# Two row tiles of a Fourier product taken by symmetry, through device memory, in batches 2 and 3

## The chip, the cores and the metric

The kernel runs on one core of one Trainium2 chip. The metric is the device time of one execution in microseconds (us), the median over runs. Before the change it is 284.78 us (three runs, 284.77 to 284.88). A difference of under 0.2% isn't told from no change.

The engines are named as in the profile: PE is TensorE (PEld its weight loads), DVE is VectorE, ACT is ScalarE, POOL is GpSimd, SP is the queue of SyncE, which here issues nearly all DMAs. Each engine runs its own instructions strictly in program order and waits at the first one whose inputs aren't ready.

## What is computed

Sparse causal attention over 4 batches of 8 heads (768 positions, head size 64), and then, for each batch, a Fourier mixing layer with an MLP:

```python
# x: (4, 768, 512), the attention's output with its heads side by side
X = np.fft.fft(x, axis=1)
X = np.fft.fft(X, axis=2)
mixed = np.real(X).astype(np.float32)
u = x + mixed
mu = np.mean(u, axis=-1, keepdims=True)
var = np.mean((u - mu) ** 2, axis=-1, keepdims=True)
un = (u - mu) / np.sqrt(var + 1e-06)
ch = np.maximum(un @ w_ch1, 0.0) @ w_ch2
return (u + ch).astype(np.float32)
```

Since `x` is real, the real part of its two-dimensional transform has a symmetry: `mixed[s, d]` equals `mixed[-s mod 768, -d mod 512]`. Row 768-s is row s with its columns 1 to 511 in reverse.

## The kernel before

The work is cut into small items, and a long string, `ORDER` (line 114), lists them one after another. The kernel walks through the list and issues the instructions of each item; so the list fixes, for each engine, the order of its own instructions. The table `WORK` (line 824) gives the function of each name. A second string, `PLACES` (line 185), says which of four PSUM buffers each new product takes, in the order in which the list makes them. An item that takes a buffer waits until the last reader of the product before it is done.

The 16 pairs of heads are numbered 0 to 15, four to a batch. A pair P goes through these items (the second number is a tile):

- `Lq`, `Lk`, `Lv`: loads on SP (line 284). `tq`, `tk` turn q and k, on PE for pairs 0 to 6 and on DVE from pair 7 on. `ks`, `kh` (block sums), `kc`, `qc`, `qs` (casts), `g` (gate scores on PE), `gt`, `gx`, `gl`, `gm` (the mask, on DVE), `K` (the mask put beside q, on POOL).
- `s:P,i`: a tile of scores on PE (line 483). `e:P,i`: its exp, on ACT (line 511). `d:P,i`: the causal diagonal, on POOL (line 519).
- `vc` (cast of v, POOL), `v:P` (attention times v, 42 matmuls, line 525), `x:P` (division into `x_b`, DVE).

A batch b is 768 rows, six row tiles of 128. After its four pairs it goes through these:

- `fs`, `fd`, `f`, `fc`: foldings of `x` on DVE and POOL. `y:b,h,gg`: the first Fourier product on PE (line 595). `ty:b,h`: its copy to SBUF, on ACT (line 614). `tr:b,h`: the same, turned, on DVE (line 622).
- `m:b,kp`: the second Fourier product, two row tiles (2 kp and 2 kp + 1) by eight matmuls of 256 columns (line 627). Row tiles 0 to 2 read `ty`, row tiles 3 to 5 read `tr`.
- `u:b,kt`: adds `x` to row tile kt of the product, into an fp32 tile in SBUF (DVE, line 640); it also sums the row. The three tiles of a batch, of two row tiles each, come from a ring of five buffers and later become the output.
- `nm:b,kt,n` (means of n row tiles, ACT), `xu:b,kt` (the centred row tile in fp16, ACT), `un:b,kt` (line 675: for batches 1 to 3 a transposing DMA on SP from `x_b` into `unT`), `bn`, `nv`, `nr` (the variance).
- `w:b,it`: a tile of the first MLP product on PE, over all 768 rows: for each of four slices of the inner dimension a matmul of 512 columns (row tiles 0 to 3) and one of 256 (row tiles 4 and 5) (line 709). `r:b,it`: its relu, on ACT or DVE (line 722). `c:b,st,h`: half of the second MLP product of row tile st, eight matmuls of 512 columns (line 731). `o` (DVE, line 753) adds it to `u`; `od` (SP, line 759) sends the row tile out.

While a batch is in its Fourier and MLP part, the pairs of the next batch fill the gaps. For batch 3 no pairs are left: between its Fourier product and its first `w` stand only the `c` items of batch 2.

Of the kernel before, what the change touches and what calls it, by code (L numbers as in the profile page):

```python
# [119 lines left out]
d:1,4 e:1,2 d:1,2 kc:4 kc:3 v:0 x:0 s:1,3 e:1,3 d:1,3 Lq:4 tq:4 qc:4 fs:0,1 s:2,2 g:3 s:1,5 e:2,2  # L120
gt:3 gx:3 gl:3,0 gl:3,1 s:2,1 e:1,5 Lv:1 vc:1 qs:4 s:2,5 e:2,1 d:1,5 d:1,1 d:2,2 e:2,5 d:1,0 d:2,5
g:4 gt:4 s:2,0 e:2,0 gx:4 gm:3 Lk:5 tk:5 s:2,3 ks:5 s:2,4 d:2,1 kh:5 d:2,0 e:2,3 d:2,3 Lq:5 tq:5
qc:5 qs:5 gl:4,0 fs:0,0 gl:4,1 Lv:2 e:2,4 d:2,4 vc:2 kc:5 v:1 x:1 s:3,2 e:3,2 Lv:3 vc:3 s:3,4 g:5
gt:5 gx:5 gm:4 fs:1,0 gl:5,0 e:3,4 d:3,4 s:3,3 s:3,0 e:3,0 s:3,5 e:3,5 d:3,5 d:3,2 d:3,0 e:3,3 d:3,3
v:2 gl:5,1 x:2 fs:2,0 fs:2,1 gm:5 fs:1,1 fd:2,1 fd:2,0 s:3,1 e:3,1 d:3,1 W:1 s:4,1 e:4,1 s:4,2 s:4,3
e:4,3 e:4,2 v:3 x:3 fs:3,1 fs:3,0 fd:3,1 fd:3,0 f:0,1 fc:0 f:0,0 s:4,5 s:5,2 e:5,2 e:4,5 d:4,5 s:4,0
e:4,0 d:4,0 s:5,0 e:5,0 LT:0 Lq:6 Lk:6 s:5,1 tk:6 ks:6 e:5,1 d:4,2 d:5,2 d:4,3 s:4,4 e:4,4 d:5,1
y:0,0,0 y:0,0,1 ty:0,0 kc:6 f:0,2 f:0,3 y:0,1,0 y:0,1,1 ty:0,1 tr:0,0 tr:0,1 s:5,3 e:5,3 s:5,4 e:5,4
LF:0 m:0,0 u:0,0 nm:0,0,1 xu:0,0 u:0,1 nm:0,1,1 m:0,2 s:5,5 e:5,5 u:0,4 nm:0,4,1 xu:0,1 u:0,5
nm:0,5,1 m:0,1 u:0,2 u:0,3 xt:0,0 tq:6 qc:6 xt:0,1 un:0,0 W:0 Lv:4 vc:4 d:4,1 kh:6 d:4,4 d:5,0 v:4  # L130
xu:0,4 xt:0,4 nm:0,2,1 xu:0,5 xt:0,5 un:0,2 g:6 gt:6 xu:0,2 nm:0,3,1 xu:0,3 xt:0,2 xt:0,3 w:0,6,2
# [745 lines left out]
```

## Time and profile before

| | before |
|---|---|
| median of the runs | 284.78 us |
| the profiled execution, its own time | 284.69 us |
| its span, from the first to the last instruction | 283.0 us |
| mean granted clock of TensorE | 0.999 |
| PE busy | 273.7 us, 2593 matmuls |
| DVE, ACT, POOL busy | 190.8, 166.3, 120.7 us |

How to read it: the profile's times count from the start of the span, so a term worked out from them is set against 283.0; the execution as a whole took 1.69 us more. The engines' busy times overlap. A line such as L636 is a line of the kernel; `out<-in` names what the instruction writes and reads, and x24 counts it. A group's line gives busy time, mean duration of one in ns, and behind the bar the idle time of the engine ahead of it with what ended it. A view by stretches gives the busy time of each engine between two moments. Matmuls are pipelined: one is shown for longer than it holds the engine, so the distance from a start to the next start is what it costs.

### The profile page before, as it was taken

The numbers are of one execution on the slowest core, as the hardware profiler recorded it, in microseconds if no ns is written. First come the engines' busy times: TensorE is split into PE (matmuls) and PEld (weight loads), VectorE is DVE, ScalarE is ACT, GpSimd is POOL, SyncE is SP. The second block draws the span as 40 slices with busy tenths as digits, with TensorE's granted clock in tenths as the row PEclk, the third lists the DMA queues.
The fourth block names the chain that finished last, engine by engine and source line by source line (L and its number), as shares of the span: only waits on it lengthen the run. The fifth ranks groups of instructions, "written<-read, shape, count | busy, mean of one in ns | idle before, by whom it ended". The sixth has DMA issues, their size and how long they took to land.

```text
span 283.0 us, 6718 instructions
## 1 busy us (share of the span) xinstructions
PE 273.7 (97%) x2593; PEld 170.0 (60%) x2593; DVE 190.8 (67%) x570; ACT 166.3 (59%) x222; POOL 120.7 (43%) x313
## 2 busy tenths in 40 slices
PE   7799998999999999999999999999999999999995
PEld 3567676876656646565665574566576555665453
DVE  2789998998899797998988669550376443380032
ACT  3599899668787269886497634669641261343100
POOL 2157839306895658747546538701522000002000
PEclk9999999999999999999999999999999999999999
DMA  7999999996999999459795152610000042000044
GB/s 179 231 218 212 222 189 154 182 189 115 156 136 203 150 131 211 63 107 193 153 205 108 28 161 74 120 71 0 0 3 2 30 110 46 2 37 0 2 166 169
DMA packets 119152, 33.45 MB, mean 118 GB/s; under 512 B 110736, under 2 KB 115920, under 8 KB 119120
## 3 DMA queue, kind: packets, MB, share of 16 engines
q1 hardware_dynamic: 113712, 28.43, 50.7%
q0 software_dynamic: 3664, 4.19, 9.6%
q10 hardware_dynamic: 1744, 0.40, 0.7%
q8 instruction: 20, 0.33, 0.5%
q14 instruction: 12, 0.10, 0.1%
HBM read 28.55 MB, written 6.29 MB: 123 GB/s over the span
## 4 chain that ended last, share of the span: by engine, by line
PE 81%; DVE 7%; DMA 3%; ACT 3%; POOL 3%; issue 2%; ACTq 0%; POOLq 0%; DVEq 0%
PE c L744 28%; PE h L719 28%; PE sc L499 7%; PE av L534 6%; PE yp L604 3%; ACT pt L516 2%; PE mx L636 2%; DMA nat<-in_k_dram 2%; PE mx L637 2%; DMA nat<-in_q_dram 1%; PE c L737 1%; DVE kr L362 1%; PE g L424 1%; PE sc L494 1%; POOL qk L246 1%
## 5 line engine op out<-in xcount | busy, mean ns | idle before, releaser
L516 ACT ACTIVATE pt<-sc 128x1024 f16<-128x1024 f32 (+1 forms) x96 | 82.8, 926 | 25.7 <-PE sc L499 17.5
L719 PE MATMUL h<-unT,w 128*128 128x256 f16 (+1 forms) x528 | 87.2, 321 | 0.0
L744 PE MATMUL c<-w_sb,hT 128*128 128x512 f16 x368 | 83.8, 379 | 0.0
L719 PEld LDWEIGHTS <-w 128*128 128x128 f16 x528 | 50.8, 98 | 31.0 <-issue 0.3
L744 PEld LDWEIGHTS <-hT 128*128 128x128 f16 x368 | 35.6, 98 | 40.2 <-issue 0.5
L729 ACT ACTIVATE hT<-h 128x768 f16<-128x768 f32 x48 | 37.8, 811 | 34.9 <-PE h L719 34.9
L522 POOL TENSOR_SCALAR_AFFINE_SELECT pt<-pt 128x256 f16<-128x256 f16 x96 | 38.0, 421 | 35.3 <-ACT pt L516 34.8
L756 DVE SCALAR_TENSOR_TENSOR u<-c,rs,u 128x512 f32<-128x512 f32 (+2 forms) x26 | 17.6, 702 | 36.4 <-PE c L744 33.3
L727 DVE TENSOR_SCALAR hT<-h 128x768 f16<-128x768 f32 x16 | 15.1, 951 | 22.0 <-PE h L719 21.9
L246 POOL TENSOR_SCALAR_AFFINE_SELECT qk<-mt 32x160 f16<-32x160 f16 x72 | 23.6, 348 | 14.1 <-DVE mt L471 12.6
L246 POOL TENSOR_SCALAR_AFFINE_SELECT qk<-q 64x768 f16<-64x768 f32 (+1 forms) x25 | 20.8, 832 | 18.8 <-DVE q L398 7.4
L499 PE MATMUL sc<-qk 96*128 96x512 f16 (+3 forms) x144 | 26.7, 306 | 0.0
L534 PEld LDWEIGHTS <-pt 128*128 128x128 f16 x672 | 22.2, 97 | 2.3 <-issue 0.7
L534 PE MATMUL av<-v,pt 128*128 128x65 f16 x672 | 23.0, 193 | 0.3 <-POOL v L246 0.3
L243 POOL TENSOR_TENSOR t<-vr,rs 128x6 f32<-128x6 f32 x12 | 2.7, 225 | 41.0 <-DVE rs L695 40.2
L499 PEld LDWEIGHTS <-qk 96*128 96x128 f16 x144 | 12.9, 98 | 9.2 <-issue 0.8
L246 POOL TENSOR_SCALAR_AFFINE_SELECT v<-nat 128x768 f16<-128x768 f32 x16 | 14.7, 922 | 5.2 <-DMA nat<-in_v_dram 5.1
L650 DVE SCALAR_TENSOR_TENSOR u<-mx,x 128x512 f32<-128x512 f32 x24 | 15.3, 683 | 2.1 <-PE mx L637 1.9
L494 PE MATMUL sc<-qk 64*128 64x512 f16 (+3 forms) x112 | 14.8, 307 | 1.9 <-ACT pt L516 0.6
L664 ACT ACTIVATE x<-u,nm 128x512 f16<-128x512 f32 x24 | 16.1, 712 | 0.3
L684 DVE BATCH_NORM_STATS2 bst<-u 128x6 f32<-128x512 f32 x24 | 16.1, 672 | 0.0
L243 DVE TENSOR_TENSOR x<-av,rcp 128x768 f16<-128x768 f32 x16 | 15.3, 958 | 0.6
(106 smaller groups left out, 318.0 us busy)
## 6 DMA issues: line engine op xcount, KB each, us to landing
nat<-in_v_dram SPq DMA_DIRECT2D x16, 384.0 KB, 5.0
out_dram<-u SPq DMA_DIRECT2D x23, 256.0 KB, 2.5
nat<-in_k_dram SPq DMA_DIRECT2D x38, 96.0 KB, 3.7
nat<-in_q_dram SPq DMA_DIRECT2D x38, 96.0 KB, 3.8
nat<-in_k_dram SPq DMA_DIRECT2D x12, 192.0 KB, 4.5
nat<-in_q_dram SPq DMA_DIRECT2D x12, 192.0 KB, 5.1
w_sb<-in_moe_w_ch_dram POOLq DMA_DIRECT2D x2, 1024.0 KB, 11.6
w<-in_moe_w_ch_dram POOLq DMA_DIRECT2D x2, 768.0 KB, 8.1
```

What stands on the lines that cost most here:

```text
L243: (eng or nc.vector).tensor_tensor(out=out, in0=in0, in1=in1, op=op)
L246: nc.gpsimd.affine_select(out=out, in_=in_, pattern=[[0, i] for i in n], base=0, channel_multiplier=0, compare_op=ALU.is_ge, fill=0.0)
L494: nc.tensor.matmul(ps[:, e, co:co + q1 - q0], qk[hs[e], 1, XW(P), 128 * jt:128 * jt + 128], qk[hs[e], 0, XW(P), q0:q1], start=(co == 0), s ...
L499: nc.tensor.matmul(ps[:, e, co:co + q1 - q0], qk[0:96, e, 1, 128 * jt:128 * jt + 128], qk[0:96, e, 0, q0:q1], start=True, stop=True)
L516: nc.scalar.activation(out=d["pt"][:, o:o + 2 * n].rearrange("p (e c) -> p e c", e=2), in_=d["sc", i][:, :, 0:n], func=AF.Exp, scale=0.125)
L522: nc.gpsimd.affine_select(out=dg, in_=dg, pattern=[[0, 2], [1, 128]], base=0, channel_multiplier=-1, compare_op=ALU.is_ge, fill=0.0)
L534: nc.tensor.matmul(av[:, e, 66 * st:66 * st + 65], pt[:, co:co + 128], vv[:, e, jt, 0:65], start=(cnt == 0), stop=(cnt == 20))
L664: nc.scalar.activation(out=x_t[b][:, kt, :], in_=u_t[b, kp][:, k2, :], func=AF.Identity, scale=0.0625, bias=u_t[b, kp, "m"][:, k2:k2 + 1])
L719: nc.tensor.matmul(hp[:, l:r], w1s, unT[:, dt, l:r], start=(dt == 0), stop=(dt == NDT - 1))
L729: nc.scalar.activation(out=hT, in_=hp, func=AF.Relu)
L744: nc.tensor.matmul(c_ps[b, g[0]][:, st - g[0], :], h_t[b, it][:, 128 * st:128 * (st + 1)], w2_t[0][:, it, :], start=(it == 0), stop=(it == ...
L756: nc.vector.scalar_tensor_tensor(out=o, in0=ps, scalar=st_t[b][1][:, st:st + 1], in1=o, op0=ALU.mult, op1=ALU.add)
```

## The change

In batches 2 and 3 (the third and the fourth) the product `m:b,2`, that is row tiles 4 and 5, isn't computed. Its rows 512 to 767 are taken from rows 1 to 256, in reverse order of rows and of columns:

- `mr:b,0` and `mr:b,1` (ACT) copy the products of row tiles 0 and 1, and the first row of row tile 2, from PSUM to an SBUF tile, with the columns reversed. Two copies each, a large one and one of two columns.
- `md:b` (SP) sends that tile to a buffer in device memory, by four DMAs: two large ones and two of one row.
- `ml:b` (SP) fetches the rows back in reverse order, by two DMAs of 128 rows of 2 KB, into the `u` tile of row tiles 4 and 5. `u:b,4` and `u:b,5` then add `x` to it in place.
- `tr` turns half of its columns in these batches, since row tiles 4 and 5 don't read it.

`ORDER` and `PLACES` are new throughout. Sorted by engine, the two lists agree up to about the item `w:0,9`, apart from the items that are new or gone.

```diff
+MIRROR = (2, 3)
...
+    dpool = ctx.enter_context(tc.tile_pool(name="turned", bufs=1, space=bass.MemoryType.DRAM))
...
     def y_turn(b, h):
         tr = bpool.tile([128, 2, S // 2], F16, tag=f"tr{h}", name=f"tr{h}_{b}")
-        nc.vector.tensor_copy(out=tr, in_=ys[b, h, 0][:, :, S // 2:0:-1])
+        n = 128 if b in MIRROR else S // 2
+        nc.vector.tensor_copy(out=tr[:, :, 0:n], in_=ys[b, h, 0][:, :, S // 2:S // 2 - n:-1])
         ys[b, h, 1] = tr
...
+    def m_rev(b, kp):
+        mps = m_ps[b, kp]
+        if b not in rev_t:
+            rev_t[b] = bpool.tile([128, 3, DM], FP, tag="zw", name=f"rev_{b}")
+        if kp == 0:
+            out, src = rev_t[b][:, 1::-1, :], mps
+        else:
+            out, src = rev_t[b][0:1, 2:3, :], mps[0:1, 0:1, :]
+        nc.scalar.copy(out=out[:, :, 511:1:-1].rearrange("p k (m two) -> p k two m", two=2),
+                       in_=src[:, :, 1:511].rearrange("p k (two m) -> p k two m", two=2)[:, :, ::-1])
+        nc.scalar.copy(out=out[:, :, 0:2], in_=src[:, :, 0:512:511])
+
+    def m_send(b):
+        rev = rev_t[b]
+        back = dpool.tile([4, 64, DM], FP, tag="back", name=f"back_{b}")
+        nc.sync.dma_start(back[1::2].rearrange("a p d -> p a d"), rev[1:65, 0:2, :])
+        nc.sync.dma_start(back[0::2, 0:63].rearrange("a p d -> p a d"), rev[65:128, 0:2, :])
+        nc.sync.dma_start(back[2, 63:64, :], rev[0:1, 0, :])
+        nc.sync.dma_start(back[0, 63:64, :], rev[0:1, 2, :])
+        rev_t[b, "d"] = back
+
+    def m_fetch(b):
+        back = rev_t[b, "d"]
+        u_t[b, 2] = u_b = bpool.tile([128, 2, DM], FP, tag="u_b", name=f"u2_{b}", bufs=5)
+        for k2 in range(2):
+            nc.sync.dma_start(u_b[:, k2, :], back[2 * k2:2 * k2 + 2, ::-1])
+
     def m_u(b, kt):
         kp, k2 = kt // 2, kt % 2
-        mps, x_b = m_ps[b, kp], x_t[b]
+        mps, x_b = m_ps.get((b, kp)), x_t[b]
...
+        if mps is None:
+            nc.vector.scalar_tensor_tensor(out=u_t[b, kp][:, k2, :], in0=u_t[b, kp][:, k2, :],
+                                           scalar=1.0, in1=x_b[:, kt, :], op0=ALU.mult,
+                                           op1=ALU.add, accum_out=st_t[b][2][:, kt:kt + 1])
+            return
...
```

The new list around the new items, sorted by engine. At the end of batch 0 and in batch 1's Fourier part (PE, DVE, POOL):

```
PE   w:0,9 s:7,5 g:9 s:8,2 v:6 s:8,3 v:7 ...
POOL K:8 d:7,3 d:7,4 kh:9 vc:6 ...
PE   m:1,0 s:9,4 c:0,4,0 c:0,5,0 g:11 c:0,4,1 m:1,2 v:9 c:0,5,1 s:10,0 s:10,4 v:8 s:11,3 g:12 s:10,1 s:11,0 s:10,3 s:10,2 w:1,12
DVE  gt:10 o:0,3 gx:10 u:1,0 tq:11 gl:10,0 u:1,1 tk:12 gl:10,1 gm:10 gt:11 ks:12 gx:11 gl:11,0 gl:11,1 tq:12 u:1,4 gm:11 u:1,5 x:9
```

In batch 2:

```
PE   m:2,0 c:1,2,0 m:2,1 c:1,4,0 s:12,4 c:1,3,0 s:12,5 c:1,3,1 s:13,0 c:1,4,1 c:1,5,0 s:13,3 s:13,4 c:1,5,1 s:13,1 c:1,2,1 s:13,5 s:14,1
ACT  mr:2,0 mr:2,1 e:12,4 nm:2,0,2 xu:2,0 nm:2,2,2 kc:15 e:12,5 xu:2,3 xu:2,2 nm:2,4,2 xu:2,4 e:13,0 xu:2,5 xu:2,1 e:13,4
DVE  o:1,1 gt:14 u:2,0 u:2,3 u:2,2 bn:2,1 gx:14 bn:2,3 u:2,4 u:2,5 bn:2,5 gl:14,0 gl:14,1 tq:15 gm:14
SP   od:1,0 md:2 ml:2 un:2,0 un:2,3 un:2,4 un:2,2 un:2,5 un:2,1
```

In batch 3:

```
PE   m:3,1 m:3,0 c:2,0,1 c:2,2,0 c:2,3,0 c:2,3,1 c:2,4,0 c:2,5,0 c:2,5,1 c:2,4,1 c:2,2,1 w:3,10 w:3,5
ACT  r:2,14 mr:3,0 mr:3,1 nm:3,0,2 xu:3,0 nm:3,2,2 xu:3,3 xu:3,1 xu:3,2 nm:3,4,2 xu:3,4 xu:3,5
SP   od:1,5 md:3 od:2,0 ml:3 un:3,0 un:3,3 un:3,1 un:3,2 un:3,4 un:3,5 od:2,3
```

More of the change, by code (lines that the diff above doesn't have):

```diff
@@ L120 @@
[L120 to L131, printed above, removed]
@@ new lines @@
+gx:2 e:1,0 Lv:1 s:1,2 d:0,3 gl:2,0 tk:4 gl:2,1 e:1,1 d:0,2 Lk:5 gm:2 d:0,0 tk:3 ks:4 d:0,5 e:1,2
+d:0,1 v:0 ks:3 kh:4 kc:4 Lq:5 kh:3 kc:3 s:1,3 x:0 qs:3 tq:4 e:1,3 d:1,4 s:2,2 d:1,2 qc:4 d:1,3 g:3
+e:2,2 fs:0,1 s:1,5 s:2,1 gt:3 vc:1 e:1,5 s:2,5 Lv:2 e:2,1 g:4 gx:3 qs:4 s:2,0 gl:3,0 e:2,5 gl:3,1
+d:1,5 e:2,0 tk:5 gt:4 d:1,1 Lv:3 d:2,2 gx:4 s:2,3 LT:0 d:1,0 s:2,4 Lq:6 gm:3 e:2,3 d:2,5 d:2,1 ks:5
+tq:5 e:2,4 v:1 qc:5 kh:5 d:2,0 kc:5 d:2,3 Lk:6 gl:4,0 fs:0,0 s:3,2 gl:4,1 qs:5 x:1 s:3,4 e:3,2 g:5
+d:2,4 vc:2 e:3,4 gt:5 s:3,3 s:3,0 gx:5 vc:3 LF:0 e:3,0 s:3,5 v:2 gm:4 fs:1,0 e:3,5 gl:5,0 d:3,4
@@ new lines @@
+xt:0,1 u:0,3 v:4 nm:0,2,1 xu:0,5 qc:6 xu:0,2 xt:0,4 un:0,0 xt:0,5 nm:0,3,1 qs:6 xu:0,3 g:6 un:0,2
+d:5,4 xt:0,2 xt:0,3 W:2 gt:6 w:0,6,2 w:0,6,0 un:0,1 d:5,3 w:0,5,2 d:5,5 gx:6 w:0,5,0 w:0,5,1 gl:6,0
+gl:6,1 gm:6 w:0,6,1 r:0,5 x:4 w:0,3 r:0,6 Lv:5 s:6,3 r:0,3 Lq:8 s:6,2 e:6,3 s:6,4 tq:7 s:6,1 e:6,4
+w:0,4,2 tk:8 w:0,4,1 e:6,2 w:0,4,0 ks:8 w:0,2 e:6,1 fs:4,0 tk:7 r:0,4 w:0,7,2 d:6,1 w:0,0 d:6,4
+r:0,2 ks:7 d:6,3 qs:7 kc:8 bn:0,0 w:0,7,1 w:0,7,0 bn:0,4 w:0,13 kh:7 r:0,0 kh:8 r:0,7 vc:5 Lc:0
+s:6,5 s:6,0 e:6,5 Lq:9 g:7 e:6,0 w:0,14 gt:7 gx:7 w:0,15 gl:7,0 r:0,14 gl:7,1 gm:7 K:7 bn:0,1 r:0,13
@@ new lines @@
+fc:1 gm:9 d:8,4 K:9 f:1,2 y:1,1,0 f:1,1 y:1,1,1 y:1,0,0 ty:1,1 bn:0,5 nv:0 nr:0 tr:1,1 y:1,0,1
+ty:1,0 tr:1,0 c:0,2,1 m:1,1 c:0,0,1 s:9,5 c:0,1,1 e:9,5 Lk:10 tk:10 ks:10 u:1,2 Lq:10 tq:10 u:1,3
+vc:8 d:8,1 qs:10 kc:10 o:0,2 s:9,1 e:9,1 s:9,2 e:9,2 o:0,0 o:0,1 Lk:11 tk:11 ks:11 c:0,3,1 kh:10
+g:10 gt:10 d:9,5 d:9,2 Lv:9 vc:9 kh:11 s:9,3 e:9,3 d:8,5 o:0,3 s:9,0 m:1,0 gx:10 u:1,0 Lq:11 tq:11
+gl:10,0 u:1,1 Lk:12 tk:12 gl:10,1 gm:10 s:9,4 c:0,4,0 c:0,5,0 od:0,2 od:0,3 Lq:12 d:8,3 d:9,3 e:9,0
+nm:1,2,2 xu:1,3 xu:1,2 un:1,2 un:1,3 nm:1,0,2 xu:1,1 un:1,1 e:9,4 xu:1,0 un:1,0 kc:11 g:11 gt:11
@@ new lines @@
+Lv:11 od:0,0 Lq:15 d:11,4 K:12 d:10,0 od:0,4 Lk:13 Lv:12 Lq:14 od:0,5 tk:13 d:10,2 e:11,2 d:11,5
+d:11,2 r:1,14 e:10,5 d:10,5 w:1,4 r:1,4 s:11,1 e:11,1 d:11,0 d:11,1 w:1,3 w:1,8 r:1,8 bn:1,1 v:10
+x:10 fs:10,0 vc:11 v:11 w:1,9 r:1,3 x:11 fs:8,0 fs:10,1 fs:11,0 fd:10,1 Lq:13 tq:13 ks:13 kh:13
+od:0,1 Lk:15 nv:1 fd:10,0 fs:11,1 fd:11,0 fd:11,1 fc:2 f:2,3 f:2,0 nr:1 Lk:14 Lv:14 vc:14 Lv:13
+r:1,9 w:1,5 s:12,3 r:1,5 w:1,1 r:1,1 w:1,6 r:1,6 c:1,0,0 s:12,2 c:1,1,0 g:13 f:2,1 tk:14 gt:13 gx:13
+f:2,2 tk:15 e:12,3 e:12,2 kc:13 c:1,0,1 s:12,1 y:2,0,0 e:12,1 y:2,1,0 y:2,1,1 y:2,0,1 s:12,0 ks:14
@@ new lines @@
+s:13,3 s:13,4 e:13,4 e:13,3 c:1,5,1 o:1,5 s:13,1 e:13,1 o:1,4 c:1,2,1 o:1,2 s:13,5 e:13,5 K:14
+s:14,1 o:1,3 g:15 gt:15 gx:15 gl:15,0 d:12,2 d:12,1 d:12,5 d:12,4 d:12,3 v:12 s:13,2 e:13,2 x:12
+fs:12,0 un:2,5 un:2,1 w:2,2 r:2,2 gl:15,1 gm:15 w:2,8 r:2,8 e:14,1 bn:2,2 w:2,7 s:14,2 e:14,2 r:2,7
+d:13,3 d:13,1 d:13,4 qs:15 d:13,2 d:13,5 v:13 s:14,4 e:14,4 x:13 K:15 s:15,3 w:2,5 r:2,5 e:15,3
+w:2,15 s:14,0 e:14,0 r:2,15 w:2,3 r:2,3 s:15,2 s:15,4 e:15,2 w:2,11 r:2,11 e:15,4 s:14,3 e:14,3
+d:14,3 Lv:15 od:1,2 d:15,4 d:14,1 d:14,2 d:15,2 od:1,4 od:1,3 w:2,12 r:2,12 s:15,0 s:15,5 e:15,5
@@ new lines @@
+w:2,10 e:15,0 s:15,1 d:15,5 d:15,0 d:14,0 s:14,5 e:14,5 d:14,4 vc:15 d:14,5 w:2,4 w:2,9 e:15,1
+d:15,1 r:2,10 r:2,4 d:15,3 v:14 r:2,9 v:15 w:2,1 r:2,1 w:2,0 r:2,0 w:2,6 r:2,6 c:2,0,0 fs:13,0
+fs:12,1 x:14 c:2,1,0 w:2,13 fs:13,1 fs:14,0 fs:14,1 x:15 fs:15,1 fd:14,0 fs:15,0 fd:15,0 bn:2,4
+fd:15,1 fd:14,1 fc:3 f:3,1 f:3,0 f:3,3 f:3,2 y:3,1,0 bn:2,0 y:3,1,1 y:3,0,0 y:3,0,1 ty:3,1 ty:3,0
+r:2,13 nv:2 nr:2 tr:3,1 tr:3,0 w:2,14 r:2,14 c:2,1,1 o:2,1 od:2,1 od:1,5 m:3,1 m:3,0 mr:3,0 mr:3,1
+md:3 c:2,0,1 o:2,0 od:2,0 u:3,3 u:3,1 u:3,0 nm:3,0,2 xu:3,0 u:3,2 c:2,2,0 c:2,3,0 c:2,3,1 c:2,4,0
@@ new lines @@
+c:2,5,0 c:2,5,1 c:2,4,1 ml:3 u:3,5 u:3,4 c:2,2,1 o:2,2 o:2,5 o:2,4 bn:3,5 bn:3,3 un:3,0 nm:3,2,2
+xu:3,3 un:3,3 xu:3,1 un:3,1 xu:3,2 un:3,2 nm:3,4,2 xu:3,4 un:3,4 xu:3,5 un:3,5 w:3,10 w:3,5 r:3,5
+bn:3,0 w:3,13 r:3,13 r:3,10 w:3,12 r:3,12 w:3,15 w:3,8 r:3,15 bn:3,1 bn:3,2 w:3,0 r:3,0 w:3,3 r:3,3
+w:3,7 r:3,7 w:3,2 r:3,2 w:3,11 r:3,11 o:2,3 w:3,4 bn:3,4 r:3,8 od:2,3 nv:3 w:3,1 r:3,4 nr:3 w:3,6
+r:3,1 r:3,6 c:3,0,0 w:3,9 c:3,1,0 r:3,9 w:3,14 r:3,14 c:3,0,1 c:3,1,1 c:3,2,0 c:3,4,0 c:3,2,1
+c:3,4,1 o:3,2 o:3,0 od:3,2 od:2,5 o:3,1 c:3,3,0 o:3,4 od:3,1 od:2,2 od:3,4 c:3,5,0 c:3,3,1 o:3,5
@@ L184 @@
+od:3,5 od:3,0 od:2,4 c:3,5,1 o:3,3 c:3,5,2 od:3,3 o:3,6 od:3,6 o:3,7 od:3,7
 """
@@ L194 @@
     "nat1": """
-0123012301231023103210320
+0123012301230123012310232
 """,
```

95 lines of the change are left out of this document (33 added, 62 removed).

## The prediction

> **What bounds the kernel now.** I read the page's first two parts and its chain of waits, then the busy time by stretches, then the waits of the matmul queue alone.
>
> ```profile
> span 283.0 us, 6718 instructions
> ...
> PE 273.7 (97%) x2593; PEld 170.0 (60%) x2593; DVE 190.8 (67%) x570; ACT 166.3 (59%) x222; POOL 120.7 (43%) x313
> ...
> PEclk9999999999999999999999999999999999999999
> ...
> PE 81%; DVE 7%; DMA 3%; ACT 3%; POOL 3%; issue 2%; ACTq 0%; POOLq 0%; DVEq 0%
> PE c L744 28%; PE h L719 28%; PE sc L499 7%; PE av L534 6%; PE yp L604 3%; ACT pt L516 2%; PE mx L636 2%; DMA nat<-in_k_dram 2%; PE mx L637 2%; DMA nat<-in_q_dram 1%; PE c L737 1%; DVE kr L362 1%; PE g L424 1%; PE sc L494 1%; POOL qk L246 1%
> ```
>
> ```profile
> core 0: us, PE busy (x) PEld busy (x) DVE busy (x) ACT busy (x) POOL busy (x), PEclk, DMA share, GB/s
> 0.00:83.00 83.00, 77.22 (x1022) 53.33 (x1023) 69.22 (x228) 64.61 (x88) 45.96 (x113) 1.00 1.01 181
> 83.00:160.00 77.00, 76.70 (x710) 45.94 (x707) 66.21 (x197) 55.41 (x73) 49.38 (x131) 1.00 0.85 145
> 160.00:212.00 52.00, 52.00 (x461) 32.62 (x458) 28.38 (x88) 29.22 (x39) 21.43 (x55) 1.00 0.24 62
> 212.00:238.00 26.00, 26.00 (x153) 14.40 (x152) 11.54 (x30) 7.48 (x12) 1.54 (x4) 1.00 0.21 51
> 238.00:262.00 24.00, 24.00 (x144) 13.97 (x143) 10.82 (x21) 8.81 (x11) 2.38 (x12) 1.00 0.03 12
> ```
>
> ```profile
> engine line waited for: us in total, times, longest us
> PE av L534 <- POOL v L246: 0.3, 1, 0.3
> ```
>
> The last fence is all that matmuls waited for between 83 and 280 us. From 83 us on TensorE is never idle beyond that, at full clock, while the other engines have room (from 160 us on about half). So there a matmul taken away is time won, and a wait put in front of a matmul is time lost, each one for one. The first 83 us are another matter (5.8 us of idle TensorE), but sorted by engine the two order lists agree up to the first half of `w:0,9`, some 82 us in, so nothing is won or lost there.
>
> **The change, part by part.** *The matmuls.* `m:2,2` and `m:3,2` go, eight matmuls each.
>
> ```profile
> 226.76 0.27 PE L636 MATMUL mx<-fd_sb,ty 128*128 128x256 f16 x1
> ...
> 227.52 0.27 PE L637 MATMUL mx<-fd_sb,tr 128*128 128x256 f16 x1
> 227.63 10.52 PE L744 MATMUL c<-w_sb,hT 128*128 128x512 f16 x48
> 237.99 2.33 PE L719 MATMUL h<-unT,w 128*128 128x512 f16 x13
> ```
>
> Eight start at 226.76 and the next work starts at 227.63: 0.87 us, so two are 1.74 us. Forty-eight matmuls of the second MLP product (`c`) take 10.36 us, so an item `c` of eight takes 1.73 us; I use that below. DVE is also spared half of four `tr` copies; it isn't the bound there.
>
> *What is added.* Per batch four copies on ACT (`mr`), four sends and two fetches on SP (`md`, `ml`). For two row tiles the adds `u` then read SBUF instead of PSUM (same count). Durations come from these groups of ACT after 83 us, the DVE add and the DMA rows:
>
> ```profile
> L516 ACT ACTIVATE pt<-sc 128x1024 f16<-128x1024 f32 x40 | 39.6, 1022 | 15.2 <-PE sc L499 12.2 <-PE av L534 2.6
> ...
> L664 ACT ACTIVATE x<-u,nm 128x512 f16<-128x512 f32 x18 | 12.0, 712 | 0.2
> ...
> L617 ACT CAST ty<-yp 128x772 f16<-128x772 f32 x6 | 6.2, 1036 | 14.4 <-PE yp L604 14.4
> ...
> L658 ACT ACTIVATE nm<-sm 128x2 f32<-128x2 f32 x9 | 1.7, 202 | 14.1 <-DVE u L650 14.1
> ```
>
> ```profile
> 226.96 0.69 DVE L650 SCALAR_TENSOR_TENSOR u<-mx,x 128x512 f32<-128x512 f32 x1 [0.78 <-PE mx L637]
> ```
>
> ```profile
> L761 SPq DMA_DIRECT2D out_dram<-u x26: 332/402/691, 106.3 to 280.2; - x26
> ...
> DMA to landing us min/median/max: 1.5/2.3/4.8
> ```
>
> ```profile
> out_dram<-u SPq DMA_DIRECT2D x1, 256.0 KB, 2.2
> ```
>
> ```profile
> out_dram<-u SPq DMA_DIRECT2D x6, 256.0 KB, 3.4
> nat<-in_v_dram SPq DMA_DIRECT2D x3, 384.0 KB, 3.5
> ```
>
> The large copy of `mr:*,0` (1020 elements a partition) has no row of its own. Below, it is an exp of 1024 elements, 1.02 us; above, `ty`, which also writes with a stride: 1.036 x 1020/772 = 1.37. I take 1.37, the row of its kind. The one-row copy of `mr:*,1` is at most an `x` of 512 (0.71), each edge copy a two-element one (0.20). `mr:*,1` with its edge is 0.9 us, both `mr` 2.5 us. A hand-over from a matmul to another engine is 0.2 us: the add at 226.96 started 0.20 us after `m:3,1` took TensorE at 226.76. The ends of the DMAs are bounded by an output tile alone on the queue (2.2 us for the same 256 KB in 2 KB rows) and the busy stretch from 140 to 175 us (3.4 out; 3.5 in, 384 KB in small pieces). I take 2.2 for a send, 1.5 for a one-row send (the fastest output), 2.5 for a fetch. So from the first send's start: the fourth send starts at 3 x 0.40 = 1.2 and lands at 2.7; the second fetch starts 0.4 later and lands at 5.6 us. The slow end is 1.2 + 3.4 + 0.4 + 3.5 = 8.5 us.
>
> A sentence on each side from the Trainium skill. "DMA: Bandwidth & Descriptors", in its section "Anatomy of one DMA", fits (for the GpSimd path) 2.0 us plus bytes/436e3 and lays most of the fixed part to the write receipt, HBM being the heaviest target: an estimate of 2.6 us for each 256 KB leg, 6.1 us in all instead of 5.6, which would lengthen both chains below by 0.5; the output row at 2.2 us is quicker than the rule. "ScalarE: Activation LUTs", in "What ACT_TABLE_LOAD costs", has 186 ns plus 0.833 ns an element: 1.04 us for the large copy, which the exp row bears out and the `ty` row (1.04 us for 772) doesn't; by it batch 3's chain would be 0.3 us shorter.
>
> *Batch 2, where it can wait.* On ACT `nm:2,4,2 xu:2,4` now stand ahead of `e:13,0`, and `s:13,4` takes the PSUM buffer that `e:13,0` reads. `nm:2,4,2` needs both fetched tiles. From the end of `m:2,1`: hand-over and `mr:2,1` 1.1, DMAs 5.6, two adds 1.4, `nm` with hand-over 0.4, `xu` 0.7, exp 1.0: 10.2 us. TensorE's cover up to `s:13,4`:
>
> ```profile
> 175.69 0.43 PE sc L499 x2
> 176.12 1.73 PE c L744 x8
> ```
>
> five `c` (8.6) and `s:12,4`, `s:12,5`, `s:13,0`, `s:13,3` (three of 0.43 and one quarter-size, 1.4): 10.0 us. A wait of 0.2 us, up to 3.1 with the slow DMAs. DVE also stands still behind `u:2,4`, with `gm:14` and so `K:14` and `s:14,1` next in line; `s:14,1` comes 4.4 us after `s:13,4`, so it yields later.
>
> *Batch 3.* All six transposes `un:3` stand behind `ml:3` on SP.
>
> ```profile
> 227.82 7.90 SPq L679 DMA_TRANSPOSE unT<-x  x6
> ```
>
> ```profile
> DMA to landing us min/median/max: 2.4/2.5/4.1
> ```
>
> Each holds SP for 7.90/6 = 1.32 us and lands 2.5 us after it starts. From the end of `m:3,0`: hand-over 0.2 and `mr` 2.5 give 2.7; the fetch may start at 5.4, or, if its tile takes the buffer that `od:2,0` empties (queued just behind `md:3`, 4.3 + 2.2), at 6.5; two issues 0.8; the sixth transpose starts 6.6 later and lands 2.5 after: 15.3 or 16.4 us. The cover is nine `c` and the first matmul of `w:3,10`, 15.5 + 0.2 = 15.7. From 0.4 spare to 0.7 short; I take 0.1. (Adds and `xu` of the fetched tiles end at 12.6 in the later case, and the sixth transpose starts at 13.9: they don't decide.)
>
> *The rest of the order.* From `w:0,9` to the end everything moves by up to 28 us, and every PSUM buffer has a new user. At 83 us the Pool wait stays: `d:7,3` now precedes `kh:9` and `vc:6`, so `g:9` waits instead, but `s:8,2` is done by then. The tightest place I find is batch 1: between `m:1,0` and `w:1,12` DVE has, before `u:1,5`, three transposes, one sum and two row maxima,
>
> ```profile
> 101.84 0.95 DVE L362 TENSOR_REDUCE kr<-k 128x12 f32<-128x768 f32 x1
> ...
> 109.44 0.97 DVE L325 STREAM_TRANSPOSE q<-nat 128x768 f32<-128x768 f32 x1
> ```
>
> ```profile
> 160.67 0.79 DVE L447 MAX8 mx<-gt 128x8 f32<-128x8 f32 x10
> ...
> 169.78 0.28 DVE L243 TENSOR_TENSOR ltb<-gt,mx 128x120 f16<-128x120 f32 x1
> 170.10 0.34 DVE L471 STREAM_TRANSPOSE mt<-ltb 128x160 f16<-128x160 f16 x1
> ```
>
> 5.4 us, with four adds 2.8 and seven mask steps at 0.28 to 0.34, 2.2: 10.4 us; then `nm`, two `xu` and a transpose's landing, 4.3: 14.7 us against 14.8 us of TensorE work. No wait by the sum, 0.7 us if DVE is late by its usual gaps. I put 0.2 us on all such places; bounds -0.5 (the old order's small waits, 0.3 seen, go) and +1.5.
>
> **The sum.** -1.74 + 0.2 + 0.1 + 0.2 = -1.24 us. The profiled execution took 284.69 us, 1.69 beyond its span; the median shown is 284.78. The span would be 281.8, that execution 283.45, the median about 283.5.
>
> **The rivals.** *The new order costs what the matmuls give.* For it: three covers within 0.3 us of their chains, DVE 86% busy from 83 to 160 us. Against: TensorE's queue held there before with one visible wait. Upper bound 1.5 instead of 0.2: 284.8, no change. *Batch 3's transposes are late* (fetch held by `od:2,0`, transposes slowed beside it; landings up to 4.1 us, +1.6): wait 0.7 to 2.3 instead of 0.1: 284.1 to 285.7, mid 284.9. For it: SP is serial and its cover is even; against: DMA share is only 0.21 there. *Slower, through batch 2's fetch:* its sends and fetches take the 3.4 and 3.5 us of the busy stretch, the round trip is 8.5 us, and `nm:2,4,2` keeps `e:13,0`, and so `s:13,4`, for 3.1 us: 284.8 - 1.74 + 3.1 + 0.3 = 286.5. It costs from a round trip of 5.4 us on and, with the other 0.3 us, outweighs the matmuls from 6.8 us on. For it: out and in at 3.4 and 3.5 overlap in time with that stretch; against: those rows stood beside other loads, and the lone one took 2.2. *The whole gain with nothing back:* 283.0 or a little below.
>
> **How the numbers follow.** Forecast, 282.9 to 284.2 with the full gain in it: 0.65. New order: 0.13 at 284.8. Batch 3: 0.10 at 284.9, about half of it slower. Batch 2: 0.12 at 286.5 and below. A difference under 0.2% (0.57 us) can't be told from none. Faster 0.66, same 0.18, slower 0.16. The range, 282.7 to 285.5, leaves out about 0.04 below and 0.12 above.
>
> **What would show it.** Right: `m` x16 fewer; TensorE still without gaps from 83 us; `s:13,4` and `w:3,10` start with under 0.5 us of wait; sends land within 2.5 us. Wrong: a wait of matmuls `sc` on ACT `pt` near 173 us, or of `h` on the transposes near 234 us, of over 1 us; many waits of 0.2 to 0.4 us spread over 84 to 210 us; ACT copies `rev` of 2 us.

## The result, and the profile after

The changed kernel takes 311.24 us (median of 6 runs, 309.33 to 311.47), the kernel before on the same chip 284.75 (284.02 to 284.88): a ratio of 1.092, 95% interval 1.089 to 1.095. It is 26.5 us slower, where 1.2 us faster was forecast. The profiled execution took 310.57 us. Its page has in the places shown before:

```profile
span 308.9 us, 6700 instructions
...
PE 276.9 (90%) x2577; PEld 169.3 (55%) x2577; DVE 189.1 (61%) x570; ACT 169.5 (55%) x230; POOL 119.9 (39%) x313
...
PEclk9999999999999999999999975999999996799999
...
PE 66%; DMA 14%; DVE 7%; ACT 6%; POOL 2%; issue 2%; SPq 1%; ACTq 0%; DVEq 0%; POOLq 0%
```

Sixteen matmuls are gone, yet TensorE is busy for 3.2 us longer, its share falls from 97 to 90%, DMA's share of the chain rises from 3 to 14%, and the granted clock dips in two places. The busy time by stretches (length, then busy time and count of PE, PEld, DVE, ACT, POOL, the granted clock, the DMA share and GB/s) finds them:

```profile
83.00:160.00 77.00, 76.69 (x709) 47.11 (x708) 62.37 (x192) 49.33 (x65) 44.58 (x116) 1.00 0.84 145
160.00:188.00 28.00, 16.08 (x91) 7.94 (x90) 11.71 (x45) 12.45 (x21) 7.21 (x15) 0.89 0.55 80
188.00:215.00 27.00, 26.47 (x226) 15.60 (x226) 13.78 (x37) 18.66 (x24) 13.80 (x38) 0.93 0.24 65
215.00:250.00 35.00, 35.00 (x275) 20.57 (x274) 14.11 (x36) 13.48 (x21) 6.24 (x22) 1.00 0.22 50
250.00:264.00 14.00, 4.05 (x16) 1.60 (x14) 5.59 (x13) 1.54 (x3) 0.00 (x0) 0.74 0.72 67
```

Up to 160 us and from 215 to 250 us TensorE is as full as before. The loss lies in two holes, one ahead of 188 us (batch 2) and one from 250 to 264 us (batch 3). TensorE's timeline (start, duration, line, work, count, and in brackets the idle time ahead of it with what ended it) names both:

```profile
175.90 0.60 PE L502 MATMUL sc<-qk 96*128 96x384 f16 x4
188.53 1.01 PE L502 MATMUL sc<-qk 96*128 96x512 f16 x2 [12.02 <-ACT pt L519]
189.34 3.13 PE L781 MATMUL c<-w_sb,hT 128*128 128x512 f16 x8
192.30 0.60 PE L502 MATMUL sc<-qk 96*128 96x256 f16 x4
...
257.84 0.58 PE L756 MATMUL h<-unT,w 128*128 128x512 f16 x1 [6.54 <-DMA unT<-x]
261.83 6.35 PE L756 MATMUL h<-unT,w 128*128 128x256 f16 x23 [3.41 <-DMA unT<-x]
```

These are the two waits that the prediction named as signs of its failure: `s:13,4`, ready behind `s:13,3` of 175.90, on an exp of ACT, and `w:3,10` on the transposes. Behind the first, eight `c` matmuls hold TensorE from 189.34 to 192.30, 2.96 us instead of 1.73: the clock, whose granted share is 0.62 from 188 to 193 us. Now the wait is followed back. ACT and DVE in batch 2:

```profile
186.61 0.20 ACT L695 ACTIVATE nm<-sm 128x2 f32<-128x2 f32 x1 [12.66 <-DVE u L683]
186.84 0.72 ACT L701 ACTIVATE x<-u,nm 128x512 f16<-128x512 f32 x1
187.47 1.00 ACT L519 ACTIVATE pt<-sc 128x1024 f16<-128x1024 f32 x1
```

```profile
180.85 0.69 DVE L683 SCALAR_TENSOR_TENSOR u<-u,x 128x512 f32<-128x512 f32 x1 [9.65 <-DMA u<-back]
...
185.87 0.69 DVE L683 SCALAR_TENSOR_TENSOR u<-u,x 128x512 f32<-128x512 f32 x1 [4.32 <-DMA u<-back]
```

The exp at 187.47 is `e:13,0`; ahead of it stand `nm:2,4,2` and `xu:2,4`, which wait for `u:2,5` at 185.87, which waits for the second fetch. And SP's queue has the trip itself:

```profile
167.65 0.65 SPq L659 DMA_DIRECT2D back<-rev  x1
168.35 0.55 SPq L660 DMA_DIRECT2D back<-rev  x1
168.95 0.33 SPq L661 DMA_DIRECT2D back<-rev  x1
169.38 0.97 SPq L662 DMA_DIRECT2D back<-rev  x1
172.78 1.23 SPq L669 DMA_DIRECT2D u<-back  x2
174.10 8.52 SPq L716 DMA_TRANSPOSE unT<-x  x2
```

The sends start at 167.65, the fetches are issued from 172.78 on, and the adds that wait for their rows start at 180.85 and 185.87: 18.2 us from the first send to the rows of the second fetch, of which 5.1 are the sends and 13.1 the fetches. The prediction has 5.6, of which 2.7 and 2.9. The first two transposes, whose rows were ready, hold the queue for 8.52 us, where all six of this batch took 8.39 before.

### The profile page after: what moved, and what is told of

Same layout as the page of the kernel before. It is cut to its first block, busy times and chain, and to the rows that moved or that the text cites. A ratio compares the mean times of both kernels' runs of the same rounds, so it can differ in the third digit from the quotient of the medians.

```text
span 308.9 us, 6700 instructions
## 1 busy us (share of the span) xinstructions
PE 276.9 (90%) x2577; PEld 169.3 (55%) x2577; DVE 189.1 (61%) x570; ACT 169.5 (55%) x230; POOL 119.9 (39%) x313
## 4 chain that ended last, share of the span: by engine, by line
PE 66%; DMA 14%; DVE 7%; ACT 6%; POOL 2%; issue 2%; SPq 1%; ACTq 0%; DVEq 0%; POOLq 0%
PE h L756 26%; PE c L781 17%; DMA u<-back 8%; PE sc L502 6%; PE av L537 5%; ACT pt L519 4%; PE yp L607 3%; DMA out_dram<-u 2%; DMA back<-rev 1%; DMA nat<-in_q_dram 1%; DMA nat<-in_k_dram 1%; PE c L774 1%; PE g L427 1%; PE tp L349 1%; DVE tr L628 1%
## 5 line engine op out<-in xcount | busy, mean ns | idle before, releaser
L756 PE MATMUL h<-unT,w 128*128 128x256 f16 (+1 forms) x528 | 90.2, 327 | 9.9 <-DMA unT<-x 9.9
L781 PE MATMUL c<-w_sb,hT 128*128 128x512 f16 x368 | 85.1, 383 | 0.0
L756 PEld LDWEIGHTS <-w 128*128 128x128 f16 x528 | 51.6, 99 | 43.4 <-issue 9.5
L695 ACT ACTIVATE nm<-sm 128x2 f32<-128x2 f32 (+1 forms) x15 | 3.0, 197 | 33.5 <-DVE u L683 26.6
L683 DVE SCALAR_TENSOR_TENSOR u<-u,x 128x512 f32<-128x512 f32 x4 | 2.7, 690 | 29.0 <-DMA u<-back 29.0
```

Source lines behind the costliest of these rows:

```text
L756: nc.tensor.matmul(hp[:, l:r], w1s, unT[:, dt, l:r], start=(dt == 0), stop=(dt == NDT - 1))
L781: nc.tensor.matmul(c_ps[b, g[0]][:, st - g[0], :], h_t[b, it][:, 128 * st:128 * (st + 1)], w2_t[0][:, it, :], start=(it == 0), stop=(it == ...
```

## The experiments

**How many DMA engines carry a fetch.** Of each fetch the device side is `[2, 64 reversed, 512]`: two groups. DMA work over 163 to 190 us in 40 slices of 0.675 us (mean busy tenths of the 16 engines, then GB/s) shows in the changed kernel

```profile
DMA  0000198019852000001111491199111115600081
GB/s 0 0 0 0 67 382 328 12 46 185 209 215 103 18 0 0 9 6 49 49 39 52 116 156 52 49 52 59 52 52 52 52 49 113 111 0 0 0 165 30
```

from the nineteenth slice on, 175 to 185 us, a share of one tenth at some 50 GB/s wherever the transposes add nothing: two engines of sixteen would be 0.125. The theory is that the number of groups sets the number of engines. The first two kernels cut the fetch into 16 groups of 8 and 4 groups of 32 reversed rows, all else as changed; the rows then land in another order than the reference's.

```
-            nc.sync.dma_start(u_b[:, k2, :], back[2 * k2:2 * k2 + 2, ::-1])
+            nc.sync.dma_start(u_b[:, k2, :], back[2 * k2:2 * k2 + 2]
+                              .rearrange("a (c p) d -> (a c) p d", c=8)[:, ::-1])
```

(`c=2` in the second.)

> The changed kernel with one pattern altered: each fetch reads the 128 rows as 16 groups of 8, each group in reverse order, instead of 2 groups of 64. Bytes, number of DMAs, sends and order stay; the rows of the mirrored half come in another order, so row tiles 4 and 5 of batches 2 and 3 are not the reference's. Theory (a fetch whose slowest dimension is 2 is carried by 2 of the 16 DMA engines): the two fetches land within 3 us of their issue instead of 7.9 and 12.4 us; what stays is the sends' 5.1 us, so the round trip is about 8.5 us and the waits fall from 12.2 to about 2.8 us at s:13,4 and from 11.5 to about 1.7 us at the first w of batch 3; no half clock; 286 to 290 us. Rival (reading rows back from device memory just after they were written is slow by itself): the fetches still take over 7 us and the time stays above 300 us.

> As the run before, with 4 groups of 32 rows. Row order again not the reference's. Theory: 4 engines, each at the same rate as before, so the two fetches take half of 7.9 and 12.4 us less the fixed part: about 4 and 6.5 us from issue to landing; 292 to 298 us. Rival: no change from 7.9 and 12.4 us, over 305 us.

Measured with 16 groups: 290.59 us, ratio 1.0225 (1.019 to 1.026); with 4 groups 301.96 (one run). Both lie above their bands, by 0.6 and 4.0 us. The same DMA view of the kernel with 16 groups, then of the one with 4:

```profile
DMA  0000991097640000799970005453627259849604
GB/s 0 0 0 0 355 382 52 0 203 152 246 146 30 0 0 27 212 331 282 161 153 0 0 0 113 81 123 72 135 59 149 46 130 260 191 136 361 258 9 188
```

```profile
DMA  0000396029851000119992222290001817273629
GB/s 0 0 0 0 149 376 252 12 85 167 237 206 70 12 0 0 12 30 211 113 107 103 100 103 100 83 194 8 0 0 28 167 41 154 53 142 66 128 62 225
```

SP's issue and DVE's first add, with 16 groups and then with 4:

```profile
172.32 1.21 SPq L669 DMA_DIRECT2D u<-back  x2
```

```profile
175.80 0.69 DVE L684 SCALAR_TENSOR_TENSOR u<-u,x 128x512 f32<-128x512 f32 x1 [5.10 <-DMA u<-back]
```

```profile
172.67 1.28 SPq L669 DMA_DIRECT2D u<-back  x2
```

```profile
178.42 0.69 DVE L684 SCALAR_TENSOR_TENSOR u<-u,x 128x512 f32<-128x512 f32 x1 [7.36 <-DMA u<-back]
```

From the issue to the add of the first 256 KB: 8.1 us with 2 groups, 5.8 with 4, 3.5 with 16, with the same sends and bytes. The trace's semaphore records agree: a fetch lands in two marks with 2 groups, in four with 4, in sixteen with 16. The theory holds, and reversed rows as such are not slow. The Trainium skill states this rule ("DMA: Bandwidth & Descriptors", in "Why a DMA increments its semaphore by 16 and not by 1"): the number of engines is the largest one up to 16 that divides the slowest dimension of both sides. The trace agrees: the share of 0.1 with two groups, 0.2 with four, 0.7 to 0.9 with sixteen.

The bands were missed for two reasons. At some 50 GB/s for two engines and 100 for four, 256 KB take 5.2 and 2.6 us, so about 3 us stay whatever the number of engines (an estimate from these rows), while the expectation for 4 groups halved nearly the whole fetch. And no half clock was expected; it followed the waits that were left at `s:13,4`, 3.2 us with 16 groups and 7.2 with 4. With 16 groups the kernel is still some 6 us slower than before; its sends, from 167.15 to the first fetch at 172.32, take 5.2 us as in the changed kernel.

**The kernel without its trip.** Two kernels leave out the sends and replace the fetch, by a GpSimd memset and by two plain loads of 128 rows of an input (the edit shown).

```
-            nc.sync.dma_start(u_b[:, k2, :], back[2 * k2:2 * k2 + 2, ::-1])
+            nc.sync.dma_start(u_b[:, k2, :], q[b, k2:k2 + 2]
+                              .rearrange("e (p r) d -> (e p) (r d)", r=12)[0:128, 0:DM])
```

> The changed kernel without the four sends and two fetches of a batch; GpSimd fills the tile of row tiles 4 and 5 with zeros in their place, so these rows of batches 2 and 3 lack the Fourier term. The matmuls left out, the ACT copies and the new order stay. Theory (all of the loss is the round trip): 283.0 to 284.2 us, the 1.74 us of the matmuls with small waits of the order. Rival (the new order costs by itself): over 285 us, with waits spread over 84 to 210 us.

> The changed kernel without its trip through device memory: the four sends are left out, and each of the two fetches is a plain load of 128 rows of 2 KB from an input, which waits for nothing but its buffer; row tiles 4 and 5 of batches 2 and 3 therefore do not hold the reference's values. The missing products, the reversing copies and the new order all stay. Theory (the whole loss is the trip): no wait at s:13,4 and none at w:3,10, and 283.2 us by the prediction's terms without its two waits (284.8 - 1.74 + 0.2), with 283 to 284.5 as the band; earlier, the kernel with a GpSimd memset there gave 288.3, of which 2.9 us was a wait that the memset itself made and some 1.7 us the half clock behind it, so 283.7. Rival (the new order costs too): 285.5 or more, with the loss spread over waits that have nothing to do with row tiles 4 and 5.

The memset kernel took 288.28 us (ratio 1.012, 1.008 to 1.016), 4.1 above the theory's band. It doesn't answer the question, for it makes a wait of its own, with half clock behind it: the memset on POOL waits for `od:1,0`'s buffer, and `qs:13` and `K:13` stand behind it.

```profile
PE sc L501 <- POOL qk L248: 2.9, 1, 2.9
```

With the plain loads: 283.61 us (283.29 to 284.42, 9 runs), ratio 0.9964 (0.995 to 0.998). Two of its stretches:

```profile
160.00:188.00 28.00, 27.56 (x203) 14.81 (x202) 20.26 (x74) 20.95 (x31) 17.11 (x41) 1.00 0.46 123
...
215.00:250.00 35.00, 35.00 (x208) 19.66 (x206) 14.25 (x32) 13.44 (x22) 2.26 (x12) 1.00 0.23 61
```

No holes, full clock. So the missing products, the copies, the adds and the new order together gain 1.1 us (the kernel before, run beside it, took 284.72), where the prediction without its two waits has 1.5, and the whole loss is the trip. The two traces have the same TensorE order, so block by block the changed one's start minus this one's says where: -0.04 us at `s:13,3`, 12.14 at `s:13,4`, 13.75 at `s:13,1`, the same up to `c:2,2,1`, 20.45 at `w:3,10`, 26.73 from `w:3,12` to the end. The spans differ by 308.9 - 282.1 = 26.8.

**The length of the trip, or the place in the queue?** Batch 2's wait needs both a late fetch and `nm:2,4,2` ahead of `e:13,0`. This kernel keeps the trip and changes the order alone:

```
-ACT  ... xu:2,2 nm:2,4,2 xu:2,4 e:13,0 xu:2,5 xu:2,1 e:13,4 e:13,3 e:13,1 e:13,5 e:13,2 ...
+ACT  ... xu:2,2 e:13,0 xu:2,1 e:13,4 e:13,3 e:13,1 e:13,5 e:13,2 nm:2,4,2 xu:2,4 xu:2,5 ...
-DVE  ... bn:2,3 u:2,4 u:2,5 bn:2,5 gl:14,0 ... gm:14 ... gx:15 ...
+DVE  ... bn:2,3 gl:14,0 ... gm:14 ... gx:15 u:2,4 u:2,5 bn:2,5 ...
```

> The changed kernel with its trip untouched, but in batch 2 the consumers of the fetched tiles are queued later: on DVE u:2,4 u:2,5 bn:2,5 behind the second transposition of g:15, on ACT nm:2,4,2 xu:2,4 xu:2,5 behind e:13,2, and on SP the transposes of row tiles 4 and 5 last. Theory A (the length of the trip decides): the 12.2 us at s:13,4 go, but the first matmul that needs those rows, w:2,2, stands only 7.1 us of TensorE work behind s:13,4, at about 183.4, while the second fetch lands at 185.9 and its four more steps need some 5 us; so 7 to 8 us of wait come back at w:2,2 with a little half clock behind them, and the time is 304 to 306. Theory B (the place in the queue decides, the trip would be hidden once nothing stands behind it): no wait at w:2,2, all 14.4 us of batch 2 gone, 296 to 298. Batch 3 is unchanged under both.

It took 307.23 us (one run). On TensorE:

```profile
182.93 0.60 PE L500 MATMUL sc<-qk 96*128 96x512 f16 x2
189.47 0.59 PE L754 MATMUL h<-unT,w 128*128 128x512 f16 x1 [5.94 <-DMA unT<-x]
191.18 5.01 PE L754 MATMUL h<-unT,w 128*128 128x256 f16 x16 [1.12 <-DMA unT<-x]
```

The wait at `s:13,4` is gone, and 7.1 us of it are back at `w:2,2`, with half clock behind; against the plain loads batch 2 still loses 9.8 us of 13.8. So the time is near what theory A has, 1.2 us above its band, but part of its path is another: the first and longer wait at `w:2,2` is on columns 0 to 511, which don't need the fetched rows at all. The transposes of the ready row tiles stand behind the fetch on SP and land between 186.3 and 189.3 us, after the second fetch at 185.7. The changed kernel has the same in batch 3; SP's queue there:

```profile
242.74 1.10 SPq L669 DMA_DIRECT2D u<-back  x2
243.94 16.61 SPq L716 DMA_TRANSPOSE unT<-x  x6
```

Six transposes take 16.61 us of the queue, where they took 7.90. The first four have their rows long before; the first takes 5.5 us to issue, and the trace has them all landed between 256.1 and 257.7 us, just behind the second fetch at 255.6. `w:3,10` starts at 257.84. So the transposes queued behind these fetches land only after them, ready or not. With 16 groups the first two also land just behind the second fetch (0.5 and 1.0 us), but that is there at 176.6. What on the chip holds them back was not tested.

**A trip that all engines carry.** The last three kernels turn the rows in another way. The copies `mr` no longer swap the two row tiles; one send of 512 KB and a single row go out in plain order, and two gathers by an index tile (256 - p and 128 - p) bring the rows back turned.

```
+        back = dpool.tile([257, DM], FP, tag="back", name=f"back_{b}")
+        nc.sync.dma_start(back[0:256].rearrange("(k p) d -> p k d", k=2), rev[:, 0:2, :])
+        nc.sync.dma_start(back[256:257], rev[0:1, 2, :])
...
+            nc.gpsimd.indirect_dma_start(u_b[:, k2, :], None, rev_t[b, "d"],
+                                         bass.IndirectOffsetOnAxis(ap=turn[:, k2:k2 + 1], axis=0))
```

> A trip that all DMA engines carry in both directions: one send of 512 KB in plain order and one row, and the rows turned by two gathers of 128 rows each with an index tile, issued by GpSimd behind K:13; and on ACT e:13,0 xu:2,1 e:13,4 e:13,3 are ahead of nm:2,4,2. It computes all of the reference. Theory (the number of engines set the trip): the send lands within 3 us of its issue and a gather within 3.5 us of its own, so the rows are there at about 175 to 176 in batch 2 instead of 185.9; s:13,4 does not wait, w:2,2 waits 0 to 1 us, batch 3 waits 0 to 3 us ahead of w:3,10, and the time is 283 to 288. Rival (the way through device memory is slow whatever the pattern, or a gather is no faster than the reversed rows): gathers of 6 us or more, and over 293.

It took 293.91 us, ratio 1.033 (1.029 to 1.037): slower than the 288 at most that was expected, and by its time alone in the rival's range, though the trip in batch 2 is short. Its DMAs to and from the turned tile, then batch 2's adds, then the two longest waits of matmuls (the first in batch 3, the second in batch 2):

```profile
L664 POOL DMA_INDIRECT u<-back,turn x4: 949/1014/1095, 172.2 to 234.2; - x4
L657 SPq DMA_DIRECT2D back<-rev x2: 377/377/377, 168.4 to 227.6; - x2
...
DMA to landing us min/median/max: 2.8/3.6/6.4
```

```profile
175.71 0.84 DVE L679 SCALAR_TENSOR_TENSOR u<-u,x 128x512 f32<-128x512 f32 x1 [3.75 <-DMA u<-back,turn]
177.31 0.69 DVE L679 SCALAR_TENSOR_TENSOR u<-u,x 128x512 f32<-128x512 f32 x1 [0.75 <-DMA u<-back,turn]
```

```profile
PE h L752 <- DMA unT<-x: 4.6, 1, 4.6
PE sc L500 <- POOL qk L247: 1.4, 1, 1.4
```

Both sends have landed 2.8 us after the first one's start (the four took 5.0), and a gather in batch 2 lands 3.5 to 3.7 us after its own start; the rows are there 8.9 us after the first send instead of 18.2. So the way through device memory is not slow whatever the pattern. In batch 3 the gathers run beside the transposes and take up to 6.4 us, after waiting for `od:2,0`'s buffer. The next kernel treats these places by order and buffer alone:

```
-POOL K:13 ml:2 kh:15 d:12,0 qs:14
+POOL K:13 kh:15 d:12,0 qs:14 ml:2
-PE   w:2,2 w:2,8 ... w:3,10 w:3,5 w:3,13
+PE   w:2,2[0:512] w:2,8[0:512] w:2,2[512:768] w:2,8[512:768] ... (w:3,10 w:3,5 w:3,13)[0:512] (w:3,10 w:3,5 w:3,13)[512:768]
-            u_t[b, 2] = u_b = bpool.tile([128, 2, DM], FP, tag="u_b", name=f"u2_{b}", bufs=5)
+            u_t[b, 2] = u_b = rev_t[b]
-        nc.sync.dma_start_transpose(un_t[b][:, :, 128 * kt:128 * kt + 128], x_t[b][:, kt, :])
+        (nc.scalar if (b, kt) == (3, 5) else nc.sync).dma_start_transpose(
+            un_t[b][:, :, 128 * kt:128 * kt + 128], x_t[b][:, kt, :])
```

(the tile of `rev` in batch 3 alone).

> The kernel with the two gathers, all of the reference computed, with the trip's remaining 8 to 9 us covered by order alone. Batch 2: the gathers stand behind qs:14 on GpSimd (in the run before they stood ahead of it, and TensorE then waited 1.4 us for GpSimd's qk), u:2,4 u:2,5 bn:2,5 behind gm:14 on DVE, and the first two blocks w:2,2 and w:2,8 compute columns 0 to 511, which need only row tiles 0 to 3, ahead of columns 512 to 767. Batch 3: the gathers write the reversed copy's own tile, so they don't wait for od:2,0's buffer (1 us); u:3,0 u:3,1 and their transposes are ahead of o:2,0; the transpose of row tile 5 is issued by ACT (1.3 us saved); and three blocks compute columns 0 to 511 first (2.6 us of TensorE work more ahead of the first use). Theory (the kernel loses only what of the trip is not covered): the 4.6 us of wait in batch 3 and the 3.6 us lost in batch 2 shrink to at most 1 us together, and the time is 283.3 to 285, at best the 283.6 of the kernel with plain loads. Rival (gathers and transposes hinder each other on the DMA engines, so that a shorter queue only makes the gathers later): over 3 us of wait left in batch 3 and 287 or more.

It took 286.17 us, ratio 1.005 (1.003 to 1.007), 1.2 us above the band. In these places no wait of over 0.5 us is left, so the rival is out (the gathers of batch 3, beside transposes, still take 4.3 and 4.8 us, but they are covered). What remains, counted block by block against the plain loads, is 0.6 us at `s:14,1` (just behind `s:13,5`), 0.4 at `w:2,2`, 1.2 from `w:3,10` to `w:3,13`. The last kernel edits those: `e:13,1` ahead of `xu:2,5`, `un:3,5` back on SP, `w:3,13` whole.

> The run before with three edits at the waits it left, the whole of the reference computed: on ACT e:13,1 ahead of xu:2,5, since s:14,1 had waited 0.4 us for it; the transpose of batch 3's row tile 5 back on SP, since ACT's began only when SP's had landed; and w:3,10 and w:3,5 alone split into two parts, w:3,13 whole, since its slot was not yet read out (0.4 us). Theory (286.2 us was the 283.6 of the kernel with plain loads plus 2.2 us of TensorE time counted block by block at s:13,5, w:2,2, w:3,10 and w:3,13): of these 0.6 us stay for the split blocks and 0.2 to 0.5 for a late transpose, and the time is 284.3 to 285.0, level with the kernel before. Rival (the trip's traffic costs something spread over the kernel that the waits don't show): 285.5 or more, with no wait of over 0.3 us left.

It took 284.47 us (12 runs, 283.62 to 285.70), ratio 1.0003 (0.999 to 1.002): level with the kernel before (284.35, run beside it). The longest wait of matmuls left in the two places is

```profile
PE h L756 <- DMA unT<-x: 0.7, 1, 0.7
```

and against the plain loads it loses 0.4 us at the split blocks of batch 2 and 0.86 from `w:3,10` to `w:3,12`. No version was found that beats the kernel before beyond what a measurement can tell; the nearest to a bound is the 283.6 of the plain loads, which make no trip at all.

## Why the prediction was wrong

*The bound: right, and the matmuls as far as shown.* Sixteen matmuls are gone; their 1.74 us were not measured alone. TensorE stood full outside the two holes, and each block that waited moved all behind it one for one: 26.73 us at the blocks, 26.8 in the span.

*The step that failed: "I take 2.2 for a send, 1.5 for a one-row send (the fastest output), 2.5 for a fetch".* The fetch was priced by rows of other DMAs of the same size, an output tile and a load of 128 partitions each, as if bytes and row length made the price. Its own pattern has two groups in front, and two engines carry it: 8.1 us for the first, 13.1 for both. Even the "slow end" of 3.5 came from rows of that other kind, so the range could not hold the time. The sends were priced too low as well, but by less: 5.1 us until the first fetch instead of 2.7. The last to land is the second large one, of 63 partitions, 4.3 us after its start instead of 2.2; the one-row sends take 3.0 to 3.2 us instead of 1.5, the price of a 64 KB piece of the output. In the gather kernel the same rows, as one DMA of 128 partitions and one row, have landed after 2.8. The pattern of the fetch stands in the diff; the prediction does not ask how many groups it has.

*Batch 2: place right, size wrong.* The chain through `nm:2,4,2`, `e:13,0` and the PSUM buffer of `s:13,4` is the one predicted, and the third rival even has the right sign. With a trip of 18.2 us in place of 5.6, the predicted chain of 10.2 us becomes 22.8; less its cover of 10.0 that is 12.8, against 12.2 measured. About 0.6 is also what the first of the two adds takes (0.7), which was done while the second fetch was still under way. The large copy of `mr:*,0` took 1.09 us, not 1.37:

```profile
L652 ACT COPY rev<-mx x4: 605/846/1091, 166.5 to 236.9; 128x1020 f32<-128x1020 f32 x2, 1x510 f32<-1x510 f32 x2
```

Here the rule of the Trainium skill ("ScalarE: Activation LUTs", in "What ACT_TABLE_LOAD costs") that was weighed, 1.04 us, was nearer than the row of `ty` that I took.

*Batch 3: place right, mechanism incomplete.* `w:3,10` waits on the transposes behind `ml:3`. But the prediction has each transpose at 1.32 us of SP and thinks the fetched tiles off the path ("they don't decide"). In fact the transposes of the four ready tiles land only behind the second fetch, and those of the fetched tiles come after: 20.45 - 13.75 = 6.7 us and then 6.3, 13.0 instead of 0.1. The fetch itself begins when `od:2,0` has landed (242.7 us), the later of the prediction's two cases.

*Not foreseen at all: the clock.* After each hole TensorE ran at half clock for a while (0.50 granted from 258 to 264 us). Of batch 2's 13.8 us this is 1.6 (13.75 - 12.14). Of batch 3's 6.3 it is at least 2.5: the matmul at 261.83 starts 24.23 us later than with the plain loads, and 26.73 is reached without another wait.

*The rest of the order:* 0.2 us with bounds -0.5 and 1.5. The plain loads gain 1.1 us by the medians; if the matmuls give 1.74, the order and what it carries cost about 0.6 (0.8 by the two profiled spans, 283.0 and 282.1). The bounds held, and the rival "the new order costs what the matmuls give" is out: 283.61 measured without the trip, where the prediction without its two waits had 283.2.

## What to carry to other kernels

Before a transfer is priced by a row of the same size, look at the outermost dimension of both its sides: 256 KB took 3.5 us in sixteen groups and 8.1 in two, and the transposes issued behind the narrow ones landed only after them. A trip that gives 0.9 us of TensorE back per batch can pay only if its whole chain is covered; here even a trip carried by all engines needed some 9 us of cover and ended level. When a wait's place is found but its length rests on a row of another pattern, the range should go up to where that length decides, not to the slowest row at hand.

## What the runs showed of the hardware that was not expected

A short idle time of TensorE can be followed by half clock. In the first gather kernel a wait of 1.4 us at 183.09 was followed by

```profile
183.00:184.20 1.20, 1.08 (x12) 0.44 (x11) 0.13 (x1) 0.00 (x0) 1.13 (x5) 1.00 0.48 96
184.20:187.60 3.40, 3.18 (x48) 2.40 (x45) 1.92 (x18) 0.00 (x0) 3.34 (x8) 0.57 0.73 49
```

first 1.2 us of full clock, then a granted clock of 0.57 over 3.4 us: against the plain loads the wait of 1.4, with one of 0.2 behind it, cost 3.4 us at `w:2,2` in all. Waits of 2.9 us (the memset) and 3.2 us (16 groups) were followed by 0.66 from 174 to 179 us and 0.59 from 179 to 183. The kernels whose waits in these places stayed under 0.8 us show none of it. But the length of the wait alone does not decide: with 16 groups a wait of 1.9 us ahead of 244.21, in batch 3, was followed by full clock.

```profile
244.00:248.00 4.00, 3.79 (x24) 2.35 (x25) 2.48 (x7) 0.81 (x1) 0.00 (x0) 1.00 0.00 0
```

The Trainium skill ("TensorE: Matmul & The Clock Gate", Part 1) gives the gate a window of about 3.4 us of idleness; the holes of 12 and 6.5 us agree with that, but the waits of 1.4, 2.9 and 3.2 us are shorter, so in these runs the clock dropped without so long an idle stretch. Why 1.4 us brought the drop and 1.9 us did not was not tried.
